# Linear attention and a two-layer MLP on one core: causal score blocks for seven pairs, one more pair in half-size products, and a new list of steps for the first stages

## The chip, the core and the metric

The kernel runs on one core of a Trainium2 chip. Its time is the device time of one execution in microseconds (us), the median of several runs; lower is better. The engines are named as in the profile: PE is TensorE's matrix unit and PEld its weight loads, DVE is VectorE, ACT is ScalarE, POOL is GpSimd, SP is SyncE, here a queue of transfers.

## The reference

Inputs `r`, `k`, `v` have shape (4, 8, 768, 48): batch, heads, time, head size. For every batch and head a 48 x 48 state is carried over time:

```
for t in range(S):
    kt, vt, rt = (k[:, :, t].copy(), v[:, :, t].copy(), r[:, :, t].copy())
    cur = np.einsum('bhd,bhe->bhde', u[None] * kt, vt)
    y[:, :, t] = np.einsum('bhd,bhde->bhe', rt, state + cur)
    state = w[None, :, :, None] * state + np.einsum('bhd,bhe->bhde', kt, vt)
```

The result, as 3072 tokens of 384 values, goes through `h = x @ w_in` (384 x 2048), `max(0.01 h, h)` and `@ w_out` (2048 x 384).

## The kernel before, in words

The 3072 tokens are 24 **stages** of 128, six to a batch (`NC`); two stages make a **pair** `m` (stages 2m and 2m+1). For each stage the recurrence is written as masked attention within the stage plus a product with the state that the stage before left.

- `prep` (letter P): r and k times powers of the decay (L318, or L325 and L327 for stages under 8). `turn` (T): PE transposes in eight matmuls (L388), ACT copies them out as `tp` (L395); from stage 8 on a DMA on SP's queue transposes (L320).
- `a_mm` (A): the scores, 128 x 128 for each of 8 heads, by `PE.matmul` (L408). Keys lie on PSUM's partitions, queries along the row; a head's 48 rows sit at partition 0 or 64, so two heads run on two halves of PE's rows. `a_mask` (M) masks them, with a product (L426) under stage 8, and from 8 on with a predicated copy (L418) into a tile that holds the diagonal already. That diagonal, the bonus `u`, comes from `bonuses` (B, L348 to L354) and `diag_tile`: on POOL (L370) for stages 8 to 11, on ACT (L376) from 12 (`LED`). Under stage 8 it comes through `diag` (X, L332) and `prep2` (Q, L340).
- `kv_mm` (K): k times v (L442); under stage 8 also the bonus columns (L438) and, as one matmul with the identity, the old state (L447). `state` (S): the new state, a product with the decay (L492), or from stage 8 on an addition and a product (L495, L497).
- `y_part` (Y): the stage's output, 16, 28 or 40 matmuls with 32 weight columns on four column groups (L527), copied to `xT` by ACT (L542).
- The first MLP product of a pair: eight groups J of six matmuls (`g1_pair`, L572), each with an ACT leaky ReLU (L578); stage by stage as G (L555).
- The second product: `g2` (H, L589) with 16 matmuls of 384 columns a stage; or `g2_seven`, which treats the pair's product as a 2 x 2 block product in seven half-size products of eight matmuls of 192 columns (L653) instead of eight, with sums of weights (`w_sum`, Z, L609) and of activations (`g_sum`, L627) on DVE, copies by ACT (L661, L677) and additions by DVE (L684). `SEVEN` holds the pairs treated so: 3 to 11.

The order of the work is written out. `ORDER` lists steps by letter and stage ("A4" is `a_mm(4)`), `LOADS` the loads that POOL's queue issues first (k, r, v of a stage, quarters of w_in and w_out). Then a loop over pairs m = 3 to 11 (`FIRST // 2` on) runs: J of pair m, scores and masks of stages 2m+4 and 2m+5, Y of 2m+2 and 2m+3, K, and the second product of pair m-1. `Sched.add` records each instruction with what it reads and writes; each engine plays its own in the order recorded and waits on semaphores for the others. Nothing is reordered at run time. PSUM's eight banks are handed out in turn by `next_bank`. F is a filler matmul, C, W, U and V prepare decay and bonus tables.

## Time and profile before

| what | value |
|---|---|
| time, median of 3 runs | 166.37 us (166.37 to 166.47) |
| span of the profiled execution, first to last instruction | 164.3 us |
| PE busy / PEld busy | 158.6 / 134.3 us |
| DVE busy / ACT busy / POOL busy | 124.1 / 120.5 / 77.0 us |
| share of the chain that ended last: PE / DVE / ACT | 93% / 4% / 1% |
| bytes moved by DMA | 19.68 MB |

The profile is one execution, and its own time is given as its span; the times are of executions without a profile. Busy time of PE counts a matmul from its start to its modelled end, and matmuls overlap, so 97% busy does not mean that no time is lost. The chain of waits follows the work back from the last instruction: each piece is what the next one had to wait for.

### The profile page before, as it was taken

The numbers are of one execution on the slowest core, as the hardware profiler recorded it, in microseconds if no ns is written. First come the engines' busy times: TensorE is split into PE (matmuls) and PEld (weight loads), VectorE is DVE, ScalarE is ACT, GpSimd is POOL, SyncE is SP. The second block draws the span as 40 slices with busy tenths as digits, with TensorE's granted clock in tenths as the row PEclk, the third lists the DMA queues.
The fourth block names the chain that finished last, engine by engine and source line by source line (L and its number), as shares of the span: only waits on it lengthen the run. The fifth ranks groups of instructions, "written<-read, shape, count | busy, mean of one in ns | idle before, by whom it ended". The sixth has DMA issues, their size and how long they took to land.

```text
span 164.3 us, 5453 instructions
## 1 busy us (share of the span) xinstructions
PE 158.6 (97%) x2315; PEld 134.3 (82%) x2315; DVE 124.1 (76%) x245; ACT 120.5 (73%) x285; POOL 77.0 (47%) x93
## 2 busy tenths in 40 slices
PE   5989899999999999999999999999999999999993
PEld 3858678788657875889889899899899899898993
DVE  7798938646999999986998997778989467045253
ACT  3767587789113869989989989989899836828530
POOL 7999999992099997750840921910000000000000
PEclk9999999999999999999999999999999999999999
DMA  4999999999999999999994995996208102002023
GB/s 96 127 152 166 172 150 171 179 196 145 148 124 246 114 126 102 214 169 84 178 128 80 195 103 110 157 110 133 90 4 193 34 4 96 4 7 89 4 96 96
DMA packets 99259, 19.68 MB, mean 120 GB/s; under 512 B 92322, under 2 KB 99236, under 8 KB 99236
## 3 DMA queue, kind: packets, MB, share of 16 engines
q0 software_dynamic: 76512, 10.03, 95.9%
q1 hardware_dynamic: 21682, 9.11, 27.5%
q8 instruction: 18, 0.29, 0.7%
q10 hardware_dynamic: 1042, 0.20, 0.6%
q14 instruction: 5, 0.04, 0.1%
HBM read 20.45 MB, written 4.72 MB: 153 GB/s over the span
## 4 chain that ended last, share of the span: by engine, by line
PE 93%; DVE 4%; ACT 1%; issue 0%
PE ps_all L572 37%; PE ps_all L653 26%; PE ps_all L589 10%; PE ps_all L527 7%; PE ps_all L408 4%; PE ps_all L388 2%; PE ps_all L442 2%; DVE at L426 2%; PE ps_all L254 1%; PE ps_all L294 1%; PE ps_all L466 1%; DVE vs L340 1%; ACT tp L395 1%; PE ps_all L555 1%; ACT gT L578 0%
## 5 line engine op out<-in xcount | busy, mean ns | idle before, releaser
L572 PE MATMUL ps_all<-xT,w_in_sb 128*128 128x256 bf16 x564 | 64.9, 273 | 0.0
L572 PEld LDWEIGHTS ps_all<-xT,w_in_sb 128*128 128x128 bf16 x564 | 54.3, 98 | 7.0 <-issue 0.2
L578 ACT ACTIVATE gT<-ps_all 128x512 bf16<-128x512 f32 x94 | 53.9, 596 | 5.8 <-PE ps_all L572 3.0
L217 POOL DMA_DIRECT2D rk_sb<-in_k_dram x23 | 21.3, 926 | 21.7 <-PE ps_all L572 21.7
L376 ACT ACTIVATE at<-ident,s_tok 128x128 bf16<-128x128 bf16 x96 | 30.4, 392 | 1.0 <-DVE s_tok L354 1.0
L418 DVE CAST_PREDICATED at<-mask,ps_all 128x1024 bf16<-128x1024 uint16 x16 | 18.8, 1220 | 5.3 <-PE ps_all L408 5.3
L217 POOL DMA_DIRECT2D v_sb<-in_v_dram x24 | 22.3, 934 | 0.8 <-POOLq L860 0.8
L684 DVE TENSOR_TENSOR out_sb<-ps_all,snap 128x192 f32<-128x192 f32 x28 | 9.9, 356 | 16.5 <-PE ps_all L653 15.8
L217 POOL DMA_DIRECT2D rk_sb<-in_r_dram x23 | 21.3, 926 | 0.0
L653 PE MATMUL ps_all<-tw,gs 128*128 128x192 bf16 x216 | 20.6, 246 | 0.0
L653 PEld LDWEIGHTS ps_all<-tw,gs 128*128 128x128 bf16 x216 | 18.1, 98 | 0.0
L589 PE MATMUL ps_all<-w_out_sb,gT 128*128 128x384 bf16 x96 | 16.4, 326 | 0.0
L653 PE MATMUL ps_all<-w_out_sb,gT 128*128 128x192 bf16 x144 | 14.9, 246 | 0.0
L627 DVE TENSOR_TENSOR gs<-gT 128x1024 bf16<-128x1024 bf16 x18 | 12.3, 684 | 2.9 <-ACT gT L578 2.9
L542 ACT ACTIVATE xT<-ps_all 128x384 bf16<-128x384 f32 x24 | 11.0, 492 | 4.2 <-PE ps_all L527 3.9
L589 PEld LDWEIGHTS ps_all<-w_out_sb,gT 128*128 128x128 bf16 x96 | 9.1, 98 | 5.8
L661 ACT ACTIVATE snap<-ps_all 128x192 f32<-128x192 f32 x27 | 9.0, 332 | 4.9 <-PE ps_all L653 4.3
L370 POOL TENSOR_TENSOR at<-ident,s_tok 128x512 bf16<-128x512 bf16 x8 | 8.7, 1131 | 7.5 <-DVE s_tok L354 7.5
L527 PE MATMUL ps_all<-at,v_sb 128*32 128x128 bf16 x384 | 11.9, 224 | 0.2 <-DVE vs L340 0.2
L653 PEld LDWEIGHTS ps_all<-w_out_sb,gT 128*128 128x128 bf16 x144 | 11.8, 98 | 0.3
L426 DVE TENSOR_TENSOR at<-ps_all,mask 128x512 bf16<-128x512 f32 x16 | 10.3, 685 | 2.1 <-PE ps_all L408 2.1
L527 PEld LDWEIGHTS ps_all<-at,v_sb 128*32 128x32 bf16 x384 | 9.1, 98 | 2.6 <-issue 0.9
(80 smaller groups left out, 220.0 us busy)
## 6 DMA issues: line engine op xcount, KB each, us to landing
out_dram<-out_sb SPq DMA_DIRECT2D x22, 192.0 KB, 2.3
v_sb<-in_v_dram POOLq DMA_DIRECT2D x24, 96.0 KB, 5.2
rk_sb<-in_r_dram POOLq DMA_DIRECT2D x23, 96.0 KB, 5.1
rk_sb<-in_k_dram POOLq DMA_DIRECT2D x23, 96.0 KB, 5.2
w_in_sb<-in_moe_w_in_dram POOLq DMA_DIRECT2D x4, 384.0 KB, 6.5
w_out_sb<-in_moe_w_out_dram POOLq DMA_DIRECT2D x4, 384.0 KB, 10.6
out_dram<-out_sb SPq DMA_DIRECT2D x4, 96.0 KB, 1.6
tp<-qk SPq DMA_TRANSPOSE x16, 3.7
```

Of the source, the lines that this page charges most:

```text
L217: add("pool", lambda: G.dma_start(dst, src), R=pace, W=[key], dma=f"{which}{n}")
L376: add("act", lambda h=h: A.activation(at[ia][:, h % 2, h // 2, :], ident[:, :], AF.Copy, scale=s_tok[n % 4][:, h:h + 1]), R=["ident", ("s" ...
L418: add("dve", lambda: V.copy_predicated(at[n % NAT][:, :, :, :].rearrange("p two m i -> p (two m) i"), mask[:, :].bitcast(mybir.dt.uint16). ...
L426: add("dve", lambda hh=hh, part=part: V.tensor_tensor(at[n % NAT][:, hh, :, :], part, mask[:, :].unsqueeze(1).to_broadcast([128, NP, 128]) ...
L527: last = PE.matmul(ps_y[32 * q:32 * q + 32, 128 * s:128 * s + 128], a, m, start=first_mm, stop=last_mm)
L542: add("act", lambda: A.activation(xT[m % NX][:, :, 128 * half:128 * half + 128], ps_y[:, 0:HD].rearrange("p (s t) -> p s t", t=128), AF.Copy),
L572: last = PE.matmul(ps_g[:, 256 * f:256 * f + 256], w_in_sb[:, s, 128 * fb:128 * fb + 128], xT[ix][:, s, :], start=s == 0, stop=s == NSL - 1)
L578: add("act", lambda: A.activation(gT[ig][:, 2 * j:2 * j + 2, :].rearrange("p f t -> p (f t)"), ps_g[:, :], AF.Prelu, alpha=0.01), R=[key], ...
L589: last = PE.matmul(ps_o[:, 0:HD], gT[ig][:, s, 128 * half:128 * half + 128], w_out_sb[:, s, :], start=s == 0, stop=s == NFB - 1)
L627: add("dve", lambda: V.tensor_tensor(x[i][:, :, :], a, b, op), R=keys, W=[("gs", m % 2, i)])
L653: done = PE.matmul(ps_o[:, 0:NH], lhs[:, s, :], rhs[:, s, :], start=first and s == 0, stop=s == HF - 1, skip_group_check=not (first and last))
L684: add("dve", lambda: V.tensor_tensor(out_sb[io][:, cols], ps_o[:, 0:NH], snap[i2][i][:, :], ALU.add), R=[key, ("snap", i2, i), *after], W= ...
```

## The change

Seven things change.

1. **Scores in causal blocks.** For the pairs (8, 9), (10, 11) to (20, 21) the odd stage is held with its two halves of 64 tokens exchanged (`SWAPPED`). Its loads and its stores become two half transfers each, and it gets its own decay table and mask. `a_blocks` makes the scores of both stages in one run of 32 matmuls on four 64 x 64 tiles of PE (row half by head, column half by keys), leaving out the blocks in which no key comes before a query. In the stage in natural order the first 64 keys meet all 128 queries and the last 64 keys only 64; in the exchanged stage it is the other way round. The order of the 32 is written by a small reckoning with 9 an issue, 56 for a 128-query product and 29 for a 64-query one.
2. **Pair 2 in seven half-size products**, its steps placed singly in the list (N2.0 to N2.6, its sums O2.0 to O2.3).
3. **States added by VectorE**: stages under 8 take the addition and product too, but for stage 7, which keeps the identity matmul as a step of its own (R7).
4. **A new list** of steps, which now reaches through J of pair 3 and the second product of pair 2; the loop runs from m = 4. Halves of P, T and M are placed singly, and J groups in any order.
5. **A new list of loads**: k3 before r2, later stage 4, weights of w_out in another order; r and k of a stage are loaded apart from v (l, v).
6. **Diagonal tiles** of stages 8 and 9 are made by ACT (E), of 10 and 11 by POOL (D).
7. Stores of whole stages (I), a skip of banks (b), and the tables for exchanged stages (t, m) become steps.

The core of the diff; left out are the table allocations, the keys by halves, and steps that are only handed on:

```diff
@@ -21,13 +21,17 @@
 NFB = DFF // 128
 NSL = HD // 128
 
-FIRST, EARLY = 6, 2
-LOADS = """r1 k1 wi0 id r2 k2 tri v1 r3 k3 v2 wi1 k4 r4 v3 wi2 k5 r5 r6 k6 v4 v5 k7 wi3 r7 v6 v7 wo3 wo2 wo1 wo0"""
+FIRST, EARLY = 8, 2
+SWAPPED = (9, 11, 13, 15, 17, 19, 21)
+LOADS = """r1 k1 wi0 id k3 tri r2 k2 v1 r3 v2 wi1 v3 wi2 k4 r4 k6 k5 r5 r6 k7 v4 v5 wi3 v7 r7 v6 wo0 wo2 wo1 wo3"""
 ORDER = """
-P0 C F1 T0 P1 F1 T1.0 A0 T1.1 X0 M0 K0 W F1 V A1 Q0 X1 S0 Y0 M1 G0.0 K1 P2 T2 Q1 P3 Y1 T3 S1 X2 A2 M2 K2 G1.0 X3 A3 U J0.2 S2 Q2 M3 Y2 K3 P4
-T4 Q3 J0.3 S3 Y3 J0.4 J0.5 J1.0 P5 A4 J1.1 P6 X4 M4 T5 X5 J1.2 K4 Q4 A5 S4 T6 J1.3 K5 J1.4 Y4 M5 L8 Q5 Y5 P7 J1.5 A6 J0.6 J2.0 J2.1 T7 M6 X6
-X7 K6 J2.2 J2.3 A7 S6 J2.4 J2.5 L9 Q6 J0.7 J1.6 J2.6 M7 Z0 Z1 Z2 L10 J2.7 L11 J1.7 K7 S7 P8 Q7 P9 B8.9 H0 K8 H1 P10 L12 K9 H2 S8 S9 Y6 Y7 A8
-A9 P11 M8 H3 M9 L13
+F1 P0.0 P0.1 C T0.0 T0.1 X0 A0 F1 K0 P1.0 F1 W M0.1 P1.1 T1.1 M0.0 Q0 T1.0 Y0 A1 P3.1 G0.0 S0 P2.0 X1 T2.0 P2.1 K1 M1.0 M1.1 T3.1 Q1 P3.0 T2.1 Y1 S1
+T3.0 X2 A2 M2.0 X3 G1.0 M2.1 A3 V K2 J0.3 Q2 M3.1 J0.2 S2 M3.0 K3 Y2 l8.3 J0.5 Q3 P4.1 P4.0 S3 P5.1 U Y3 P6.1 T4.1 T4.0 J0.4 J1.2 A4 P5.0 T5.1 J1.3
+M4.1 P6.0 X4 M4.0 T5.0 J1.4 T6.1 J1.1 X5 K4 J1.0 K5 v8.3 P7.1 Q4 T6.0 A5 S4 Y4 T7.1 J1.7 M5.1 M5.0 Q5 P7.0 X6 J0.6 Y5 v9.25 l9.33 A6 T7.0 v10.31 M6.1
+K6 J2.5 A7 M6.0 J0.7 Q6 S6 M7.1 J2.2 J2.0 J2.1 J2.6 X7 J2.4 M7.0 t l10.22 K7 Z0 Z2 Z1 P8 J1.5 J1.6 J2.3 J2.7 Q7 Z3 B8.9 E8.4.5 v11.33 E9.2.3 l11.20 H1
+m H0 R7 P9 E8.2.3 S7 I1 H2 O2.0 Y6 l12.2 E8.0.1 E9.0.1 E9.4.5 O2.2 Y7 K9 K8 O2.1 P10 S8 P11 E8.6.7 H3 l13.32 J3.4 S9 B10.11 E9.6.7 A8 M8 J3.3 D10 M9
+J3.7 O2.3 J3.0 I0 J3.1 B12.13 v13.22 v12.24 D11 I3 J3.6 J3.2 I2 l14.30 J3.5 E12.0.1 l15.40 A10 Y8 M10 P13 E13.6.7 Y9 P12 N2.0 N2.1 E13.4.5 K10 v14.24
+N2.2 S10 E13.0.1 b1 N2.3 E12.2.3 E12.4.5 N2.4 v15.24 E13.2.3 N2.5 M11 E12.6.7 N2.6
 """
 
 
...
@@ -138,8 +142,13 @@
     NQK, NTP, NVS, NAT, NT, NX, NG, NO, NRK = 6, 6, 6, 6, 6, 3, 3, 4, 14
     TURNED, DIAG = 8, 8
     LED = 12
-    SEVEN = (3, 4, 5, 6, 7, 8, 9, 10, 11)
+    SEVEN = (2, 3, 4, 5, 6, 7, 8, 9, 10, 11)
     HF, NH = NFB // 2, HD // 2
+    HL = L // 2
+    SWAP = SWAPPED
+
+    def swapped(n):
+        return n in SWAP
     w_in_sb = SB("w_in_sb", [128, NSL, DFF])
     w_out_sb = SB("w_out_sb", [128, NFB, HD])
     rk_sb = SB("rk_sb", [128, NRK, 2, HD])
...
@@ -213,8 +226,18 @@
...
-        key = (which, n if which == "v" else n % NRK)
-        add("pool", lambda: G.dma_start(dst, src), R=pace, W=[key], dma=f"{which}{n}")
+        slot = n if which == "v" else n % NRK
+        if swapped(n):
+            for half in range(2):
+                to, of = slice(HL * half, HL * half + HL), slice(HL - HL * half, L - HL * half)
+                add("pool", lambda to=to, of=of: G.dma_start(dst[to], src[of]), R=pace, W=[(which, slot, half)],
+                    dma=f"{which}{n}{half}")
+            return
+        add("pool", lambda: G.dma_start(dst, src), R=pace, W=[(which, slot, 0), (which, slot, 1)], dma=f"{which}{n}")
+
+    def got(which, n):
+        slot = n if which == "v" else n % NRK
+        return [(which, slot, 0), (which, slot, 1)]
 
     def load_stage(n, pace=()):
         for which in "krv":
...
@@ -358,13 +391,10 @@
         for step in range(3):
             for n in stages:
                 bonus(n, step)
-        for n in stages:
-            if n < LED:
-                diag_tile(n)
 
     def diag_tile(n, heads=range(H)):
         ia = n % NAT
-        if n < LED:
+        if heads is None:
             for hh in range(2):
                 s_of = s_tok[n % 4][:, :].rearrange("p (m two) -> p two m", two=2)[:, hh, :]
                 add("pool", lambda hh=hh, s_of=s_of: G.tensor_tensor(
...
@@ -399,6 +429,9 @@
         it = n % NTP
         if n >= DIAG and taken[0] % 8 == 7:
             taken[0] += 1
+        if swapped(n + 1):
+            a_blocks(n)
+            return
         at_bank[n] = (next_bank(), next_bank())
 
         def emit():
...
@@ -411,17 +444,48 @@
...
-    def a_mask(n):
+    def a_blocks(n):
+        stages = (n, n + 1)
+        for x in stages:
+            if taken[0] % 8 == 7:
+                taken[0] += 1
+            at_bank[x] = (next_bank(), next_bank())
+
+        def block(x, p, hh, half):
+            rows, keys = slice(64 * hh, 64 * hh + D), slice(HL * half, HL * half + HL)
+            whole = half == (1 if swapped(x) else 0)
+            queries = slice(0, L) if whole else keys
+            dst = at_bank[x][hh][0][keys, 128 * p + queries.start:128 * p + queries.stop]
+            return PE.matmul(dst, tp[x % NTP][rows, NP + p, keys], tp[x % NTP][rows, p, queries], start=True, stop=True)
+
+        def emit():
+            now, free = 0, {(hh, half): 0 for hh in range(2) for half in range(2)}
+            todo = {tile: [(x, p) for p in range(NP) for x in stages] for tile in free}
+            while any(todo.values()):
+                def turn_of(tile):
+                    return max(free[tile], now) + 2 * (tile[1] == swapped(todo[tile][0][0])), tile[0]
+
+                tile = min((t for t in todo if todo[t]), key=turn_of)
+                x, p = todo[tile].pop(0)
+                start = max(free[tile], now)
+                now, free[tile] = start + 9, start + (56 if tile[1] == swapped(x) else 29)
+                last = block(x, p, *tile)
+            return last
+
+        add("pe", emit, R=[("tp", x % NTP, half) for x in stages for half in range(2)],
+            W=[key for x in stages for _, key in at_bank[x]])
+
+    def a_mask(n, *parts):
...
-                mask[:, :].bitcast(mybir.dt.uint16).unsqueeze(1).to_broadcast([128, H, 128]),
+                (mask_s if swapped(n) else mask)[:, :].bitcast(mybir.dt.uint16).unsqueeze(1).to_broadcast([128, H, 128]),
...
-                R=[key for _, key in at_bank[n]] + ["mask"] + halves, W=halves)
+                R=[key for _, key in at_bank[n]] + (["mask_s"] if swapped(n) else ["mask"]) + halves, W=halves)
             return
-        for hh in range(2):
+        for hh in parts or range(2):
...
...
@@ -443,17 +507,18 @@
                                      qk[iq][:, H + 2 * p:H + 2 * p + 2, :].rearrange("p h e -> p (h e)"),
                                      v_sb[:, n, :].rearrange("p (h e) -> p h e", e=E)[:, 2 * p:2 * p + 2, 0:D],
                                      start=p == 0 or not carried, stop=not carried)
-            if live and carried:
-                last = PE.matmul(ps_kv[:, 0:HD], ident[:, :], st[n % NT][:, :, :].rearrange("p m e -> p (m e)"),
-                                 start=False, stop=True)
             return last
 
-        reads = [("kp", iq), ("v", n), ("qk0", iq)]
+        reads = [("kp", iq), ("qk0", iq)] + got("v", n)
         if n < DIAG:
             reads += [("prod", n % 4), "wu0", "wu1"]
-        if live and carried:
-            reads += [("st", n % NT), "ident"]
         add("pe", emit, R=reads, W=[key])
+
+    def carry(n):
+        ps_kv, key = kv_bank[n]
+        add("pe", lambda: PE.matmul(ps_kv[:, 0:HD], ident[:, :], st[n % NT][:, :, :].rearrange("p m e -> p (m e)"),
+                                    start=False, stop=True),
+            R=[("st", n % NT), "ident"], W=[key, ("carried", n)])
 
     def decay_columns():
         ps_c, key_c = next_bank()
...
@@ -590,10 +655,19 @@
...
+        add("pe", emit, R=[("gT", ig, half, j) for j in range(8)] + [("wout", i) for i in range(4)], W=[key, ("second", n)])
...
+
+    def g2_store(n):
+        io = n % NO
+        if swapped(n):
+            for half in range(2):
+                of, to = HL * half, 128 * n + HL - HL * half
+                add("sp", lambda of=of, to=to: SP.dma_start(out[to:to + HL, :], out_sb[io][of:of + HL, :]),
+                    R=[("o", io, 0), ("o", io, 1)], W=[("out", n, half)], dma=f"o{io}")
+            return
         add("sp", lambda: SP.dma_start(out[128 * n:128 * n + 128, :], out_sb[io][:, :]),
             R=[("o", io, 0), ("o", io, 1)], W=[("out", n, 0)], dma=f"o{io}")
 
...
@@ -695,6 +771,15 @@
             for n, h in tiles[lo:hi]:
                 diag_tile(n, [h])
 
+        if step is not None:
+            [lambda: (product(0, (0, 0), (top, one), True, False), keep(0, 0)),
+             lambda: (product(1, 0, 0, True, False), keep(1, 1)),
+             lambda: (product(0, 1, 1, False, False), keep(0, 2)),
+             lambda: (product(2, (0, 1), (low, one), True, True), plus(2, 0, 0, 0)),
+             lambda: (product(0, 2, 2, False, False), plus(0, 1, 1, 1)),
+             lambda: (product(1, 3, (low, two), False, True), plus(1, 2, 0, 1)),
+             lambda: (product(0, (1, 1), 3, False, True), plain(0, 1, 0))][step]()
+            return
         if not final:
             product(0, (0, 0), (top, one), True, False)
             some(0, 2)
...
@@ -739,6 +824,22 @@
...
 
+    def swapped_tables():
+        for name, own, col, turned in (("q", "qexp", qexp, qexp_s), ("k", "kexp", kexp, kexp_s)):
+            for half in range(2):
+                rows = slice(HL * half, HL * half + HL)
+                by = float((HL if half == 0 else -HL) * (1 if name == "q" else -1))
+                add("dve", lambda rows=rows, by=by, col=col, turned=turned: V.tensor_scalar(
+                    turned[rows, :], col[rows, :], 1.0, by, ALU.mult, ALU.add), R=[own], W=[(own, "s", half)])
+        for i, (own, turned) in enumerate((("qexp", qexp_s), ("kexp", kexp_s))):
+            add("act", lambda i=i, turned=turned: A.activation(tab_s[:, i, :], lnw[:, :], AF.Exp, scale=turned[:, 0:1]),
+                R=[("lnw", 0), ("lnw", 1), (own, "s", 0), (own, "s", 1)], W=[f"tab_s{i}"])
+
+    def swapped_mask():
+        add("dve", lambda: V.tensor_copy(mask_s[:, :], mask[:, :]), R=["mask"], W=["mask_s"])
+        add("dve", lambda: V.memset(mask_s[0:HL, HL:L], 0.0), R=["mask_s"], W=["mask_s"])
+        add("dve", lambda: V.memset(mask_s[HL:L, 0:HL], 1.0), R=["mask_s"], W=["mask_s"])
+
...
...
@@ -748,8 +849,16 @@
...
-    steps = {"U": u_table, "V": u_cast, "P": prep, "Q": prep2, "B": bonuses, "T": turn, "A": a_mm, "M": a_mask, "K": kv_mm, "S": state, "Y": y_part, "X": diag, "C": decay_columns, "W": decay_table, "F": fill, "Z": w_sum,
-             "G": g1, "J": g1_pair, "H": g2, "L": lambda n: load_stage(n, pace=[("pace", (n - 4) // 2, (n - 4) % 2)])}
+    def load_paced(n, after, which="krv"):
+        for one in which:
+            load_one(n, one, pace=[("second", after) if after < 10 else ("pace", after // 10 - 1, after % 10)])
+
+    def skip_banks(n):
+        taken[0] += n
+
...
+             "G": g1, "J": g1_pair, "H": g2, "L": load_paced,
+             "l": lambda n, after: load_paced(n, after, "kr"), "v": lambda n, after: load_paced(n, after, "v")}
...
...
@@ -760,34 +869,29 @@
...
-
+                g2_store(2 * m + half)
+
+    while taken[0] % 8 != 6:
+        taken[0] += 1
...
-        first = [n for n in ahead if n < LED]
-        if first:
-            bonuses(*first)
-        if first and further:
-            w_sum(3)
-            bonuses(*further)
...
-        if further and not first:
+        if further:
             bonuses(*further)
-        for n in (2 * m + 8, 2 * m + 9):
-            if n < NST:
-                load_stage(n, pace=[("pace", 2 * m, 0)])
+        for which in ("kr", "v"):
+            for n in (2 * m + 8, 2 * m + 9):
+                for one in which * (n < NST):
+                    load_one(n, one, pace=[("pace", 2 * m, 0)])
         for n in ahead:
-            if n < DIAG:
-                diag(n)
+            if not swapped(n):
+                a_mm(n)
         for n in ahead:
-            a_mm(n)
-        if not first:
-            for n in ahead:
-                a_mask(n)
+            a_mask(n)
...
```

61 lines of the change are left out of this document (36 added, 25 removed).

## The prediction

> **What bounds the kernel now.** I read the page first, then the chain of waits in order of time, then groups by line and the timeline where a term needed them.
>
> ```profile
> span 164.3 us, 5453 instructions
> PE 158.6 (97%) x2315; PEld 134.3 (82%) x2315; DVE 124.1 (76%) x245; ACT 120.5 (73%) x285; POOL 77.0 (47%) x93
> PE 93%; DVE 4%; ACT 1%; issue 0%
> ```
>
> TensorE (PE) carries 93% of the chain. The chain itself shows where it does not (start, length, what):
>
> ```profile
> 13.13 0.18 PE ps_all L447
> ...
> 15.60 1.29 DVE at L426 x2
> ...
> 18.15 1.20 DVE at L426 x2
> ...
> 21.22 0.67 PE ps_all L527 x40
> ...
> 25.09 0.60 ACT gT L578
> 25.69 0.99 ACT tp L395 x2
> ...
> 40.72 0.08 PE ps_all L438 x4
> ...
> 40.99 0.16 PE ps_all L447
> 41.15 2.60 PE ps_all L589 x16
> ...
> 58.86 0.55 PE ps_all L408 x16
> ...
> 65.89 5.24 PE ps_all L572 x48
> ...
> 73.02 4.68 PE ps_all L653 x56
> ...
> 152.50 9.32 PE ps_all L653 x112
> ```
>
> The reader is to see two regions. From 27 us to 161.8 us the chain holds nothing but matmuls, so there a microsecond of matmul time taken out is a microsecond of the end, as long as no other engine takes over. Before 27 us it leaves PE several times, longest from 15.60 to the end of Q3's and P4's steps near 19.9, where VectorE (DVE) masks, scales and adds for stages 2 and 3 while PE has too little to do. The steady loop starts pair 4 at 65.89 in this kernel; the changed list of steps ends at the same point of the work (pairs 0 to 3 through the first product, pairs 0 to 2 through the second, scores to stage 11), so I compare the two up to that point and then per loop.
>
> The span is 164.3 us; the median time is 166.37 us, so 2.07 us lie outside the span, which I leave as they are.
>
> **The change part by part.**
>
> *Pair 2 in seven half-size products.* Two products of 16 matmuls each, 2 x 2.60 = 5.20 us, become seven of 8: the row at 73.02 gives 4.68 us. Term: **-0.52 us**. On the path. It brings four sums on DVE and three additions from PSUM:
>
> ```profile
> L627 DVE TENSOR_TENSOR gs<-gT 128x1024 bf16<-128x1024 bf16 x18 | 12.3, 684 | 2.9 <-ACT gT L578 2.9
> L684 DVE TENSOR_TENSOR out_sb<-ps_all,snap 128x192 f32<-128x192 f32 x28 | 9.9, 356 | 16.5 <-PE ps_all L653 15.8 <-ACT snap L661 0.7
> ```
>
> That is 4 x 0.68 + 3 x 0.36 = 3.8 us of DVE, to be hidden; see DVE below.
>
> *States added by VectorE.* The identity matmul that carried the state into PSUM (0.16 to 0.18 us in the chain) ran five times and stays once, for stage 7: 4 x 0.165 = **-0.66 us** of PE. Four times DVE does an addition and a product instead of one product:
>
> ```profile
> L447 PE MATMUL ps_all<-st,ident 128*128 128x384 bf16 x5 | 1.6, 326 | 0.0
> ...
> L495 DVE TENSOR_TENSOR sum_t<-ps_all,st 128x384 bf16<-128x384 f32 x11 | 6.1, 551 | 0.0
> ...
> L497 DVE TENSOR_TENSOR st<-sum_t,wl 128x384 bf16<-128x384 bf16 x11 | 4.3, 394 | 0.4
> ```
>
> The product alone is the 0.39 us that each costs DVE beyond the addition, which takes the place of the old product; three of them fall in the stretch before 22 us in which DVE is on the chain.
>
> *Causal blocks.* A pair's scores are 16 products of 128 queries (first row below), and become 32 products on four tiles: per tile four of 128 queries and four of 64. No row has a 64-wide tile; the nearest is L527, four 32-column tiles side by side:
>
> ```profile
> 58.79 0.62 PE L408 MATMUL ps_all<-tp 48*128 48x128 bf16 x16
> ...
> 59.63 0.23 PE L527 MATMUL ps_all<-at,v_sb 128*32 128x128 bf16 x4
> 59.69 0.23 PE L527 MATMUL ps_all<-tp,st 128*32 128x128 bf16 x4
> 59.74 0.23 PE L527 MATMUL ps_all<-at,v_sb 128*32 128x128 bf16 x4
> ```
>
> In the first row the last product alone lasts 0.22 us, so the starts of eight twos span 0.40: one two every 56 ns, 448 ns a pair. On L527 four products start every 55 ns, so four tiles work at once, their weight loads are hidden, and an issue costs no more than 14 ns. A 64-query product should take half, some 29 ns. A tile then needs 4 x 56 + 4 x 29 = 340 ns; products issue in order, and stepping through the written order with the 9 ns an issue that the new code itself reckons with ends it at 388 ns. Gain 448 - 388 = 60 ns, or 108 at best; I take 80 ns a pair: 7 x 0.08 = **-0.56 us**. Bounds: -0.76 us (nothing lost to issue) and +3.1 us (second rival). Masks, their number and their size stay; the products still sit between two other shapes, so the gaps around them stay too.
>
> [...]
>
> *Swapped loads.* In seven stages each load becomes two half loads, 21 more issues on POOL's queue, and each store of theirs two on SP's.
>
> ```profile
> L217 POOL DMA_DIRECT2D v_sb<-in_v_dram x24 | 22.3, 934 | 0.8 <-POOLq L860 0.8
> L231 POOL DMA_DIRECT2D w_out_sb<-in_moe_w_out_dram x4 | 3.0, 824 | 0.0
> ```
>
> A w_out issue has half the rows of a v issue (512 against 1024) and still takes 0.82 us, so a half load costs nearly a whole one: 21 x 0.7 = 15 us more on POOL, which is busy 77 of 164. All come after the weights. Cost nil; the cover is POOL's idle half. Without it a load lands late for a stage two pairs on.
>
> *DVE and the diagonal tiles.* Stages 8 and 9 get their diagonal tiles from ScalarE (ACT) and no longer from POOL.
>
> ```profile
> 40.25 0.96 DVE L609 TENSOR_TENSOR tw<-w_out_sb,tw 128x1536 bf16<-128x1536 bf16 x1
> ...
> 55.06 5.25 DVE L609 TENSOR_TENSOR tw<-w_out_sb,tw 128x1536 bf16<-128x1536 bf16 x1
> 55.41 4.08 POOL L370 TENSOR_TENSOR at<-ident,s_tok 128x512 bf16<-128x512 bf16 x4
> 40.00:45.00 5.00, 5.00 (x44) 3.38 (x43) 4.97 (x12) 1.74 (x4) 0.00 (x0) 1.00 2.64 146
> 45.00:50.00 5.00, 5.00 (x86) 3.20 (x87) 4.90 (x9) 1.14 (x3) 4.43 (x4) 1.00 1.42 164
> ```
>
> DVE's difference of weights stood 5.25 us while POOL made four tiles; the same form at 40.25 took 0.96 (first row). In the new list it comes before any POOL tile, so DVE gets back about 4.3 us, which pays for the 3.8 us of sums. The 16 ACT tiles fall where ACT is busy 1 to 2 of 5 us (after the window's length stand PE, PEld, DVE, ACT and POOL, each with its count). Still, counting DVE's steps from the weight differences to the end of the list gives some 24 us of work in 24.6 us: hidden, with little to spare. What PE waits for there (masks of stages 8 and 9, transposes of 8 to 11) is due 2 to 3 us before its turn.
>
> *The early list.* DVE decides up to step Q3, which lets Y3 go:
>
> ```profile
> 8.63 1.29 DVE L426 TENSOR_TENSOR at<-ps_all,mask 128x512 bf16<-128x512 f32 x2 [0.35 <-PE ps_all L408]
> ...
> 17.61 0.55 DVE L340 TENSOR_TENSOR vs<-v_sb,ps_all 128x384 bf16<-128x384 bf16 x1
> 18.07 1.28 DVE L426 TENSOR_TENSOR at<-ps_all,mask 128x512 bf16<-128x512 f32 x2
> 19.27 0.35 DVE L325 TENSOR_TENSOR qk<-rk_sb,tab 128x384 bf16<-128x384 bf16 x1
> ...
> 19.81 0.56 DVE L340 TENSOR_TENSOR vs<-v_sb,ps_all 128x384 bf16<-128x384 bf16 x1
> 20.28 0.55 DVE L492 TENSOR_TENSOR st<-ps_all,wl 128x384 bf16<-128x384 f32 x1
> ```
>
> From the first mask at 8.63 to the end of Q3, where the next row starts at 20.28, DVE hardly rests; the starts give what a step takes of the queue (a mask pair 1.20, a scaling 0.47, a pair of decay products 0.54, a state 0.47). In the new list the steps from the first mask to Q3 are 4 x 1.20, 4 x 0.47, 3 products of L332 x 0.33, 3 x 0.54, and states 0.47 + 2 x 0.86: 11.5 us, so 20.1, and an estimated 0.4 us more because k3 and k2 land just when their steps are due. That is 20.5, about as late as before. But three J groups stand ahead of Y3 and not two (0.66 us of PE under the wait), the scores of stage 1 fill the wait for xT, and at 26 us, where ACT held the chain for 1.59 us, more J is at hand. Against this stage 4's r is loaded a place later behind k4:
>
> ```profile
> 23.34 0.36 DVE L325 TENSOR_TENSOR qk<-rk_sb,tab 128x384 bf16<-128x384 bf16 x1 [2.51 <-DMA rk_sb<-in_r_dram]
> 39.26 0.96 DVE L609 TENSOR_TENSOR tw<-w_out_sb 128x1536 bf16<-128x1536 bf16 x1 [1.38 <-DMA w_out_sb<-in_moe_w_out_dram]
> ```
>
> The loads land in a row without a break (stage 5 waited until 23.34), so in the new list stage 4 is complete near 21.8 and PE idles about 0.45 us for its transposes. Following PE's steps from Y3 (end near 21.3 instead of 21.89) to the first second product I get 39.7 instead of 41.15; 0.66 of that are the state products counted above and 0.16 the one that now comes later, so 0.6 is left: **-0.5 us** for the list. Bounds: -2.0 (nearly half of the stretch of 4.3 us at 15.60) and +1.2 us (three times 0.39 us with no J under it). It cannot gain much more: the w_out weights land near 39.2 (second row), and no second product can start before.
>
> **Sum:** -0.52 - 0.66 - 0.56 - 0.5 = -2.24 us; span 162.1, time 166.37 - 2.24 = **164.1 us**.
>
> **The rivals.**
>
> 1. *The blocks gain nothing.* A 64-query product takes as long as a 128-query one (its load shows): 8 x 56 ns a tile, as now. For it: no row has a 64-wide load. Time 166.37 - 0.52 - 0.66 - 0.5 = 164.7. [...]
>
> 2. *The loads of the tiles share one path* (the other side). Four 32-column loads fit in 55 ns, at most 13.9 ns each; if that is because they queue, a 64-column load takes 27.7 ns and 32 of them 0.89 us, +0.44 us a pair, +3.1 us in all: 166.37 - 1.68 + 3.1 = 167.8. Slower from +0.24 us a pair on, 21.5 ns a product. Against it: rows 0 to 63 and 64 to 127 of the scores already load side by side, and a two-column product with a full load takes 20 ns (40.72, four in 0.08).
>
> 3. *The early list loses.* The extra additions and a late load put Y1 to Y3 behind without J to fill: +1.2 instead of -0.5: 165.8. For it: DVE has no slack from 8.6 to 20.3 us.
>
> 4. *The list gains more*, nearly half of the stretch at 15.60: -2.0 instead of -0.5: 162.6. Against it: the weights' landing.
>
> 5. *DVE takes over between 40 and 65 us.* 24 us in 24.6 us; 2 us of stalls (POOL's four tiles stand in its way again) reach the path after the slack: +1 us, 165.1.
>
> **How the numbers follow.** Forecast 0.44, rival 1 0.14, rival 2 0.11, rival 3 0.12, rival 4 0.11, rival 5 0.08. A measurement of this kernel tells about 0.2% (0.33 us) from no change. Faster: the forecast, 1, 4, 5 and most of 3, less a share for two of them together: 0.80; same 0.05; slower 0.15. The range leaves out rival 2 and half of rival 4: 162.8 to 166.3.
>
> **What would show it.** Chain: one L447-like step; second products 5.20 us gone before the loop. Scores of stages 12 and on: about 0.47 us a pair where 0.55 stood; 0.55 means rival 1, 0.9 or more rival 2. Loop start of pair 4 near 64.1 instead of 65.89; later than 65.9 means rival 3 or 5, and the chain says where: DVE pieces before 27 us (3) or after 40 us (5). The forecast is wrong if the chain after 27 us holds more than 1 us that is not PE.

## The result, and the profile after

The changed kernel takes **168.66 us** (median of 6 executions, 168.04 to 169.66), the kernel before 166.42 beside it: 1.0141 times as long, 95% interval 1.0106 to 1.0177. A second measurement, on another chip, gave 1.0144 (1.0090 to 1.0198). Ratios, here and below, are of the means of fast executions, so they are not quite the quotients of the medians. The forecast was 164.1 with a range up to 166.3: wrong by 4.6 us, and on the wrong side.

The profiled execution took 168.14 us, of which the span is 166.4. Three lines of its page, the span, the engines, and the shares of the chain of waits:

```profile
span 166.4 us, 5784 instructions
...
PE 157.3 (95%) x2447; PEld 135.0 (81%) x2447; DVE 127.1 (76%) x263; ACT 125.4 (75%) x305; POOL 83.0 (50%) x110
...
PE 83%; DVE 5%; POOL 4%; DMA 3%; issue 2%; ACT 2%; POOLq 0%; DVEq 0%
```

PE's busy time fell by 1.3 us, from 158.6, but PE now carries 83% of the chain and not 93%. The chain in order of time (start, length, what) says where it left PE:

```profile
18.09 0.67 issue
...
24.25 0.32 issue
...
40.94 5.20 PE ps_all L654 x32
...
54.64 2.35 DVE at L482 x2
...
58.11 2.62 DVE ku L381 x2
...
61.00 0.62 DVE ku L384 x2
61.62 0.47 DVE s_tok L387
...
64.41 3.54 PE ps_all L731 x40
67.95 5.24 PE ps_all L637 x48
73.19 0.47 PE ps_all L459 x31
```

Three points of the work, the same in every kernel, cut the span into stretches: the first second product (40.94), the start of pair 4 in the loop (67.95), and the end of the last addition. The last two columns are kernels of the experiments below. All rows but the last are of one profiled execution each: 166.3 us in the column of the mended orders, 165.3 in the last.

| us | before | forecast | changed | all orders mended | the same, 38 instructions more |
|---|---|---|---|---|---|
| first second product | 41.15 | 39.7 | 40.94 | 41.92 | 41.02 |
| from there to pair 4 | 24.74 | 24.4 | 27.01 | 24.21 | 24.22 |
| pair 4 to the last addition's end | 96.31 | 95.9 | 95.96 | 95.96 | 95.95 |
| from there to the span's end | 2.1 | 2.1 | 2.5 | 2.4 | 2.4 |
| time, median | 166.4 | 164.1 | 168.7 | 165.8 | 164.8 |

So the loop gave what was forecast; 1.2 us are missing ahead of the first second product and 2.6 between there and the loop. (0.4 us more lie behind the last addition, in the stores' landing; no run was made for them.) Why the second stretch grew stands in three views. PE's waits (total, times, longest; the two rows with issue belong to the first stretch and come further below):

```profile
PE ps_all L506 <- DVE at L482: 2.1, 1, 2.1
...
PE ps_all L637 <- issue: 0.7, 1, 0.7
PE ps_all L441 <- issue: 0.3, 1, 0.3
```

L506 is K10, the state product of stage 10. It waits for a mask although it reads none: its PSUM bank is the one in which the scores of stage 10 stood (bank 7, by the order in which banks are handed out), and the mask M10 reads them. DVE's instructions in order of time show why that mask is late:

```profile
58.11 2.96 DVE L381 TENSOR_TENSOR ku<-rk_sb,u_tab 128x384 bf16<-128x384 bf16 x2
61.00 0.62 DVE L384 TENSOR_TENSOR ku<-rk_sb,ku 128x384 bf16<-128x384 bf16 x2
61.54 1.00 DVE L387 TENSOR_REDUCE s_tok<-ku 128x8 f32<-128x384 bf16 x2
62.46 1.21 DVE L482 CAST_PREDICATED at<-mask,ps_all 128x1024 bf16<-128x1024 uint16 x1
```

Step B12.13, six instructions for stages that are due a pair later, stands ahead of M10 in DVE's queue, and its first two products together take 2.96 us where the next two of the same size take 0.62. POOL in the same stretch (idle time before an instruction and what ended it, in brackets):

```profile
49.31 0.89 POOL L236 DMA_DIRECT2D rk_sb<-in_k_dram  x1 [8.39 <-PE ps_all L654]
...
58.65 2.21 POOL L400 TENSOR_TENSOR at<-ident,s_tok 128x512 bf16<-128x512 bf16 x2
60.81 0.95 POOL L236 DMA_DIRECT2D rk_sb<-in_k_dram  x1
```

While POOL makes the diagonal tiles of stage 11 (58.65 to 60.86), DVE's two products take nearly five times as long. The loads that B12.13 needs are issued from 49.31 on, held back 8.39 us by their gate (step H2, the second product of stage 2, the first of pair 1), and the last half of r of stage 13 lands at 60.70. So two causes end together at 60.7 to 60.9. Which of them counts was the first question.

### The profile page after: what moved, and what is told of

The parts are those of the page before. It is cut to its first block, busy times and chain, and to the rows that moved or that the text cites. A ratio compares the mean times of both kernels' runs of the same rounds, so it can differ in the third digit from the quotient of the medians.

```text
span 166.4 us, 5784 instructions
## 1 busy us (share of the span) xinstructions
PE 157.3 (95%) x2447; PEld 135.0 (81%) x2447; DVE 127.1 (76%) x263; ACT 125.4 (75%) x305; POOL 83.0 (50%) x110
## 4 chain that ended last, share of the span: by engine, by line
PE 83%; DVE 5%; POOL 4%; DMA 3%; issue 2%; ACT 2%; POOLq 0%; DVEq 0%
PE ps_all L637 34%; PE ps_all L731 28%; PE ps_all L592 6%; PE ps_all L654 6%; DMA rk_sb<-in_k_dram 3%; PE ps_all L506 2%; POOL rk_sb L236 2%; PE ps_all L441 2%; DVE ku L381 2%; PE ps_all L418 2%; PE ps_all L459 1%; DVE at L482 1%; ACT at L406 1%; DVE at L490 1%; POOL v_sb L236 1%
## 5 line engine op out<-in xcount | busy, mean ns | idle before, releaser
L637 PE MATMUL ps_all<-xT,w_in_sb 128*128 128x256 bf16 x564 | 65.2, 273 | 0.7 <-issue 0.7
L406 ACT ACTIVATE at<-ident,s_tok 128x128 bf16<-128x128 bf16 x112 | 35.6, 390 | 4.9 <-DVE s_tok L387 4.9
L236 POOL DMA_DIRECT2D rk_sb<-in_k_dram x16 | 14.8, 926 | 24.6 <-PE ps_all L637 16.2
L731 PE MATMUL ps_all<-tw,gs 128*128 128x192 bf16 x240 | 23.1, 246 | 0.3 <-ACT snap L739 0.3
L731 PEld LDWEIGHTS ps_all<-tw,gs 128*128 128x128 bf16 x240 | 20.0, 98 | 0.5 <-ACT snap L739 0.5
L236 POOL DMA_DIRECT2D v_sb<-in_v_dram x17 | 16.2, 960 | 0.8 <-POOLq L961 0.8
L731 PE MATMUL ps_all<-w_out_sb,gT 128*128 128x192 bf16 x160 | 16.5, 247 | 0.0
L482 DVE CAST_PREDICATED at<-mask,ps_all 128x1024 bf16<-128x1024 uint16 x9 | 10.9, 1220 | 5.5 <-PE ps_all L459 3.2
L236 POOL DMA_DIRECT2D rk_sb<-in_r_dram x16 | 14.8, 929 | 0.0
L731 PEld LDWEIGHTS ps_all<-w_out_sb,gT 128*128 128x128 bf16 x160 | 13.0, 98 | 0.5
L425 ACT ACTIVATE tp<-ps_all 128x512 bf16<-128x512 f32 x16 | 9.1, 601 | 2.8 <-PE ps_all L418 2.8
L654 PE MATMUL ps_all<-w_out_sb,gT 128*128 128x384 bf16 x64 | 10.9, 326 | 0.0
L233 POOL DMA_DIRECT2D v_sb<-in_v_dram x14 | 10.3, 791 | 0.0
```

The source lines that it names most:

```text
L236: add("pool", lambda: G.dma_start(dst, src), R=pace, W=[(which, slot, 0), (which, slot, 1)], dma=f"{which}{n}")
L406: add("act", lambda h=h: A.activation(at[ia][:, h % 2, h // 2, :], ident[:, :], AF.Copy, scale=s_tok[n % 4][:, h:h + 1]), R=["ident", ("s" ...
L482: add("dve", lambda: V.copy_predicated(at[n % NAT][:, :, :, :].rearrange("p two m i -> p (two m) i"), (mask_s if swapped(n) else mask)[:, ...
L637: last = PE.matmul(ps_g[:, 256 * f:256 * f + 256], w_in_sb[:, s, 128 * fb:128 * fb + 128], xT[ix][:, s, :], start=s == 0, stop=s == NSL - 1)
L654: last = PE.matmul(ps_o[:, 0:HD], gT[ig][:, s, 128 * half:128 * half + 128], w_out_sb[:, s, :], start=s == 0, stop=s == NFB - 1)
L731: done = PE.matmul(ps_o[:, 0:NH], lhs[:, s, :], rhs[:, s, :], start=first and s == 0, stop=s == HF - 1, skip_group_check=not (first and last))
```

## Experiments between the first second product and the loop

The theory: place in a queue is the whole of it, B12.13 ahead of M10. The rival: DVE, POOL and the DMA engines have too much to do there, and another wait takes the place of each that goes. Edits are to the list of steps unless said otherwise; ratios are to the kernel before on the same chip.

**Loads earlier, tiles earlier, both.** Gate of the loads of 12 and 13 moved from H2 to H1, which runs first of all second products (a); POOL's tiles D11 ahead of two loads of v (b); both (c).

```diff
-O2.0 Y6 l12.2 E8.0.1                     (a, c)
+O2.0 Y6 l12.1 E8.0.1
-B12.13 v13.22 v12.24 D11 I3              (b, c)
+B12.13 D11 v13.22 v12.24 I3
```

> The changed kernel with k and r of stage 12 (and so of 13 behind them on POOL's queue) released by the second-product step H1 instead of H2. My theory: in the changed kernel step B12.13 stands on VectorE until 61 us for two reasons that end together, the last half load of r13 (lands 60.7) and POOL's two diagonal tiles of stage 11 (58.65 to 60.86); mask M10 stands behind it, K10 on PE behind M10 by its bank (2.1 us) and the third of pair 2's seven products behind ACT (0.3 us). Taking away the load alone leaves POOL's tiles: I expect the loop of pair 4 to start where it did (67.95, within 0.5 us) and 168.1 to 168.7 us. If the load alone held B12.13: start near 65.7, time near 166.3. If VectorE is simply full: unchanged, 168.1 to 168.7.

> The changed kernel with POOL's diagonal tiles of stage 11 ahead of the v loads of stages 13 and 12 on POOL's queue. My theory: the tiles then run from about 56.4 to 58.5 us, under the masks of stages 8 and 9, and hold B12.13's first product no longer, but r13 still lands near 60.7: loop start unchanged within 0.5 us, 168.0 to 168.7 us. If POOL's tiles alone held VectorE: start near 65.8, time near 166.4. If VectorE is simply full: unchanged.

> Both edits: loads of stages 12 and 13 released by H1, and POOL's tiles of stage 11 ahead of the v loads. My theory (two causes that end together): only now does B12.13 run at 57 to 59.5 us; M10 follows A10 at once, K10 waits no more than 0.7 us, the loop of pair 4 starts at 65.5 to 66.2 instead of 67.95, time 166.0 to 166.8 us. If one of the two alone was the cause, the time here equals that of the run that removed it. If VectorE is simply full, start at 67 or later and 167.5 or more.

a: 170.37 us, ratio 1.0207 (1.0123 to 1.0291), above the 168.1 to 168.7 expected, because PE's clock was halved for a while in three of its four executions (mean granted clock 0.99; see under hardware); loads issued from 44.57 instead of 49.31, yet the two products of L381 take 2.96 us again, under POOL's tiles, and K10 waits 2.1 us. b: 168.17, 1.0136 (1.0066 to 1.0206); the two take 1.46, but the last L384 starts only at 61.38, behind the load of r13, whose last half lands at 61.30, and K10 waits 1.7. c: 168.40, 1.0116 (1.0058 to 1.0174); K10's wait is 0.4 and pair 4 starts near 66.7 (65.5 to 66.2 was expected, and 166.0 to 166.8 us). Either cause alone holds the mask; both must go. But c's next pair starts at 80.25, where the changed kernel had 79.69. DVE's queue in c:

```profile
73.30 0.36 DVE L384 TENSOR_TENSOR ku<-rk_sb,ku 128x384 bf16<-128x384 bf16 x1 [2.28 <-DMA rk_sb<-in_r_dram]
```

r15 came late. POOL issued the loads of 14 and 15 from 61.64, behind its tiles, and not from 60.81; the last half of r15 was issued 0.75 us later than in the changed kernel, and it landed 4.1 us later (73.22 for 69.14). Why it took so much longer is not shown. The gain was given back one pair on, as the rival has it.

**The mask first** (d): B12.13 behind M10 and the decay products, the ACT tiles that need it further back.

```diff
-J3.1 B12.13 v13.22 ... A10 Y8 M10 P13 E13.6.7 Y9 P12 N2.0 N2.1 E13.4.5 K10
+J3.1 v13.22 ... A10 Y8 M10 P13 Y9 P12 B12.13 N2.0 N2.1 K10
```

> The changed kernel with step B12.13 and the diagonal tiles of stages 12 and 13 put behind mask M10, P13 and P12 in the list (tiles on ACT behind the copy of the third of pair 2's products). Loads and POOL's order as in the changed kernel. My theory (M10 and the copies are held by what stands ahead of them in their queues): K10 waits under 0.5 us, the loop of pair 4 starts at 65.2 to 65.8 instead of 67.95; of these 2.3 us up to 1 us may be given back in the next loop, where ACT then makes 16 tiles before the first group's copies. Time 165.9 to 167.0 us. If VectorE is simply full: M10 still ends after 62 us and the time stays at 167.8 or more.

167.16 us, ratio 1.0042 (1.0018 to 1.0066): 1.0% below the changed kernel by a few steps moved, with no load, no POOL tile and no operation changed. M10 starts at 59.99, as soon as its scores are there, and K10's wait is gone; pair 4 starts at 66.77, later than the 65.2 to 65.8 asked. The next two rows are DVE's, the last is of PE's waits:

```profile
59.99 1.22 DVE L482 CAST_PREDICATED at<-mask,ps_all 128x1024 bf16<-128x1024 uint16 x1 [1.37 <-PE ps_all L459]
61.46 0.56 DVE L348 TENSOR_TENSOR qk<-rk_sb,tab_s 128x768 bf16<-128x768 bf16 x1 [0.24 <-DMA rk_sb<-in_r_dram]
```

```profile
PE ps_all L731 <- DVE out_sb L761: 0.9, 1, 0.9
```

The theory holds for the largest part. What stays is 0.9 us: DVE idles 1.37 us ahead of the mask, then takes the decay products that waited for r13, then B12.13, and the additions that free a PSUM bank come behind them.

**Loads of 14 and 15 earlier too** (e: c and this; f: d, a and this, with P13 P12 ahead of the mask and D11 ahead of the loads of v). The expectation of f calls the gates of a the first and the second half of pair 1's product; they are H1, of pair 0, and H2.

```diff
-H3 l13.32 J3.4 ... I2 l14.30 J3.5 E12.0.1 l15.40 A10
+H3 l13.32 l14.30 l15.40 J3.4 ... I2 J3.5 E12.0.1 A10
```

> The kernel with both edits (earlier loads of stages 12 and 13, POOL's tiles ahead of two loads of v) and a third: the loads of r and k of stages 14 and 15 come directly behind those of 12 and 13. If what took back the 1.3 us was only the late loads of 14 and 15 (r15 landed at 73.2 us), DVE's wait of 2.28 us for r15 goes, the next pair's first products start near 79.0 instead of 80.08, and the time is about 166.9 instead of 168.4. If it was the transposes of stages 12 and 13, started at 62.97 behind the bonus step, the wait of 1 us of the scores of stage 12 stays and the time stays within 0.4 us of 168.4.

> The order with the mask of stage 10 ahead of the bonus step (167.16 before), and beside it: loads of 12 and 13 gated by the first instead of the second half of the product of pair 1, loads of 14 and 15 behind them, POOL's tiles ahead of the loads of v, and the decay products of 13 and 12 ahead of the mask. By the theory that queue positions alone made the loss after 41 us, the remaining gap of 1.17 us on PE at 64.8 goes (the products of 13 no longer wait for r13 until 61.27), pair 4 starts near 65.6 and the time is near 165.9, below the kernel before by about 0.5 us. By the rival that DVE has too much to do between 41 and 65 us, another wait of about 1 us takes its place and the time stays near 167.

e: 167.55, ratio 1.0060 (1.0022 to 1.0098); f: 167.55, 1.0065 (1.0017 to 1.0113). In e the late r15 and K10's wait are gone and the next pair starts at 78.70, close to the 79.0 expected, though the time missed its 166.9; f missed its 165.9 by 1.6 us. Both have a new wait of PE, here in e, ahead of the scores of stages 10 and 11:

```profile
60.51 0.59 PE L459 MATMUL ps_all<-tp 48*64 48x64 bf16 x32 [1.68 <-issue]
```

The view names no releaser. By the landing times in the trace it is the DMA transposes of stage 11, on which these scores wait too: issued at 51.90 they landed at 60.42, 8.5 us later, and in f they took 8.6 (52.38 to 61.00). In the changed kernel it was 6.8 (51.90 to 58.71), and in the loop, where POOL issues no load from 75.8 to 80.8, 3.0 (77.10 to 80.15). The profile counts the packets of transposes and loads alike as shares of the same 16 DMA engines. Over all 16 transposes of e:

```profile
DMA to landing us min/median/max: 3.0/3.7/8.9
```

**Transposes earlier** (h: e, and P11 ahead of S8 on DVE), **all orders mended** (i).

```diff
-O2.1 P10 S8 P11 E8.6.7                   (h, i)
+O2.1 P10 P11 S8 E8.6.7
-J3.1 B12.13 v13.22 v12.24 D11 I3 J3.6 J3.2 I2 l14.30 J3.5 E12.0.1 l15.40 A10 Y8 M10 P13 ...   (i: also l12.1)
+J3.1 D11 l14.30 l15.40 v13.22 v12.24 I3 J3.6 J3.2 I2 J3.5 P13 P12 A10 Y8 M10 Y9 B12.13 ...
```

> The kernel with earlier loads of 12 to 15 and POOL's tiles ahead of two loads of v, and one edit more: the decay products of stage 11, behind which their transposes are issued, stand ahead of the state addition of stage 8 on DVE. In the kernel without it PE had a gap of 1.95 us before the scores of stages 10 and 11 that the trace gives no cause for; the transposes of stage 11 were issued at 51.90 and landed at 60.42, 8.5 us later, where transposes without loads beside them land after 3.0 us. By the theory that transposes share the DMA engines with the loads, issuing them about 1.7 us earlier takes most of that gap away (below 0.6 us) and the start of pair 4 moves from 66.96 to about 65.4: time about 166.0. If the gap is another thing (instructions arriving late, the banks), it stays at 1.9 us and the time is unchanged, 167.5.

> Everything together: mask of stage 10 ahead of the bonus step, loads of 12 and 13 earlier, decay products of stage 11 earlier, POOL's tiles and then the loads of 14 and 15 ahead of the loads of v. By the theory that the loss after 41 us is the place of a few steps on DVE, POOL and the DMA queues, no wait above 0.5 us is left on PE between 41 us and the loop, pair 4 starts 2.3 us earlier than in the changed kernel (about 65.6), and the time is 166.0, 0.4 below the kernel before. By the rival that DVE or the DMA engines are simply full in this stretch, a wait of about 1 us remains somewhere and the time stays at 167.

h: 166.98, ratio 1.0024 (0.9990 to 1.0058). The gap is 1.36 us from product to product (1.95 in e) where below 0.6 was expected, and the time 166.0: the transposes of stage 11 were issued 0.8 us earlier and landed at 60.43, as in e. Issued sooner, with four stages' loads ahead of them, they landed no sooner. In i those of 14 and 15 come behind POOL's tiles; the transposes issued at 51.47 land at 57.22, and no wait is left. i: **165.80, ratio 0.9945 (0.9917 to 0.9974)**, and on a second chip 165.84, 0.9947 (0.9919 to 0.9976). Its shares of the chain, and its chain:

```profile
PE 95%; issue 1%; ACT 1%; DVE 1%
```

```profile
41.92 5.20 PE ps_all L654 x32
...
59.81 0.47 PE ps_all L459 x32
...
62.77 3.37 PE ps_all L731 x40
66.13 5.24 PE ps_all L637 x48
```

From 41.92 to the last addition everything on the chain is PE, and the stretch to pair 4 takes 24.21 us. The rival is refuted: all operations of the changed kernel fit, none taken out, in another order. Beside it the changed kernel ran on that second chip (control o, 168.91), and the 1.4 to 2.0% asked of it were 1.9 by the medians, two of its six executions with the halved clock.

> The kernel with all orders mended, unchanged, as the control on the chip of the two kernels above: 165.8, ratio to the kernel before 0.9945, if what was measured holds on another chip.

> The changed kernel unchanged, as the control on the same chip: ratio to the kernel before 1.014 as measured; by the theory that its loss after 41 us is three waits that the mended orders take away, 1.4 to 2.0% above the kernel with all orders mended.

## Experiments ahead of the first second product

**A load** (g): k of stage 2 loaded ahead of k of stage 3, and stage 3's decay products behind the masks of stage 1.

```diff
-... id k3 tri r2 k2 v1 r3 ...            (loads)
+... id k2 tri r2 k3 v1 r3 ...
-A1 P3.1 G0.0 S0 P2.0 X1 T2.0 P2.1 K1 M1.0 M1.1 T3.1 Q1 P3.0 T2.1 Y1 S1 T3.0
+A1 P2.1 G0.0 S0 P2.0 X1 T2.0 K1 M1.0 M1.1 T2.1 Q1 P3.1 P3.0 Y1 T3.1 S1 T3.0
```

> The changed kernel with k of stage 2 loaded ahead of k of stage 3, and the decay products of stage 3 behind the masks and the scaling of stage 1 on DVE. By the theory that the early chain hangs on the load of k2 (landing at 12.28 us, masks right behind it), the second output product Y1 starts near 13.9 instead of 14.38; if the early stretch passes that on, the first second product starts at 40.5 instead of 40.94 and the time is 168.2 instead of 168.66. By the rival that DVE's queue and not a load sets Y3, Y1 is earlier but Y3 is not, and the time stays within 0.2 us.

170.07, ratio 1.0186 (1.0118 to 1.0255): a miss, three of its four executions with the halved clock. Y1 starts at 14.86 and not at 13.9, and PE's nameless gap grew from 0.95 to 1.22 us. No gain is seen, but the changed kernel itself has Y1 at 14.38 in one profile and at 15.03 in another (control o), as its loads land sooner or later; so one profile doesn't settle what the exchange is worth.

**The nameless gaps.** In every kernel with the new list but one (m, below) PE stops once or twice with nothing that releases it, inside a group of like products. The rows of the changed kernel, of i, of s and of l (the next experiments), in that order, each from its own view of PE:

```profile
18.76 0.71 PE L637 MATMUL ps_all<-xT,w_in_sb 128*128 128x256 bf16 x5 [0.67 <-issue]
...
24.56 0.23 PE L441 MATMUL ps_all<-tp 48*128 48x128 bf16 x2 [0.32 <-issue]
```

```profile
19.74 0.70 PE L637 MATMUL ps_all<-xT,w_in_sb 128*128 128x256 bf16 x5 [1.35 <-issue]
```

```profile
23.57 0.27 PE L418 MATMUL ps_all<-ident,qk 128*128 128x128 bf16 x2 [0.96 <-issue]
```

```profile
23.02 0.22 PE L418 MATMUL ps_all<-ident,qk 128*128 128x128 bf16 x1 [0.39 <-issue]
```

Counted in the trace's instructions of PE (weight loads, products, and the waits of its sequencer), they stand at 448 to 450 and 704 to 707 in every kernel that has them, 256 apart. The trace also holds instruction loads, 16,384 bytes each, in the page of the changed kernel this row (count, MB, share of 16 engines):

```profile
q8 instruction: 19, 0.31, 0.7%
```

256 instructions to a load make 64 bytes an instruction. If PE's instructions come in blocks, adding some early moves each gap to other work. s adds 20 two-column products (40 instructions) to the changed kernel after step C; l puts the same 20 in i in place of a filling product of the same length (0.69 us at 4.19 for 0.61 at 4.18; the expectation has 1.65 us, a misreading of the row), 38 more; m 34 of them, 66 more.

```diff
-F1 P0.0 P0.1 C T0.0 T0.1                 (l; m: f34)
+f20 P0.0 P0.1 C T0.0 T0.1
+    def small(n):   # "f": n products of 128x128 ones by two columns
```

> The changed kernel with 20 two-column products of ones put in on PE near 4.5 us, where it waits; 40 instructions of PE more ahead of everything that follows, no other change. The two gaps of PE at 17.82 us (945 ns) and 24.03 us (532 ns) end with nothing the trace names. If they are PE's instructions arriving late, they stay at the same count of instructions and so come 40 instructions earlier in the work: before the scores and state products near 16.6 to 17 us, and near 22.9 us, and none inside the groups where they stood; the time may change by up to 1.3 us either way. If they belong to the work there (operands, banks), they stay at the same products.

> The kernel with all orders mended, and in place of the first filling product (2 instructions) 20 two-column products of ones (40 instructions), at 1.65 us where PE waits for w: 38 instructions of PE more ahead of all that follows, no time of their own on the way. In all kernels so far the work passed PE's instruction 704 between 5.79 and 6.15 us after 448, whatever stood there, and the first second product came 16.38 us after 704 in the eight kernels with the new list and no instruction put in; the start of the first 16 KB instruction load varied from 13.76 us (with 40 instructions put in) to 17.43. By the theory that PE's instructions arrive in blocks of 256 and that this sets the stretch from 18 to 25 us, the first gap (1.62 us in the kernel it is made from) moves off J's products and may vanish, a gap before instruction 704 stays, 704 comes 5.8 to 6.1 us after 448, and the time moves by up to 0.7 us, most likely down to 165.2. By the rival that the gaps belong to the work, both stay at the same products and the time stays at 165.8.

> The same with 34 small products, 66 instructions more. They take some 0.9 us from 1.65 us on, as the two products they stand for did with their gaps, or 0.3 us more. By the theory of blocks of instructions: gaps, if any, at instruction 448 and 704 again, which is 66 instructions earlier in the work (near 16.1 and 22 us in the changed kernel); 448 to 704 again 5.8 to 6.1 us; time 165.0 to 166.3. By the rival: gaps at the old products, time 165.8 to 166.1.

| us | goes on at 448 (after a stop of) | at 704 (after) | those two loads start | time, ratio |
|---|---|---|---|---|
| before | 17.74 (none) | 24.02 (none) | 15.48, 21.23 | 166.42 |
| changed | 18.76 (0.95) | 24.56 (0.53) | 16.43, 21.98 | 168.66, 1.0141 |
| i | 19.74 (1.62) | 25.54 (0.53) | 17.34, 23.06 | 165.80, 0.9945 |
| i, second chip | 18.32 (0.31) | 24.40 (0.81) | 15.91, 21.66 | 165.84, 0.9947 |
| s | 17.51 (none) | 23.57 (1.18) | 13.76, 20.69 | 169.88, 1.0145 (1.0049 to 1.0240) |
| l | 17.52 (none) | 23.02 (0.60) | 12.70, 20.12 | **164.77, 0.9883 (0.9848 to 0.9919)** |
| m | 17.83 (none) | 22.88 (none) | 12.13, 19.63 | 165.40, 0.9913 (0.9878 to 0.9949) |

(Stops are from one product's start to the next.) The gaps went with the count: in s, l and m none stands inside J's products any more, and where one is left it stands at 704, now in the transposes. That they belong to the count and not to the work is shown. Every stop of the table ended 2.3 to 2.9 us after its load started, so late instructions are the likely cause; that a load's late start is due to the full DMA queues of that phase is only argued. The fixed 5.8 to 6.1 us from 448 to 704 that l and m were expected to keep fell (5.5 and 5.05): blocks have no fixed pace. What the stops cost: l takes 1.07 us less than i on the same chip (164.62 to 165.34 against 165.09 to 166.18), more than the 0.6 expected of it. (The profiles are not the medians: l's took 165.34, its longest time, that of i on this chip 165.09, its shortest.) m has no stop at all and is no faster than l: its second output product Y1 came at 16.31, after l's 15.29, behind a load of k that landed at 14.21 (12.29 in the changed kernel). Counted from Y1, the stops account for the rest: to the first second product it takes 25.2 us in m, 25.7 in l, 26.6 in the changed kernel and 27.2 in i, and with their stops taken off (0, 0.60, 1.48 and 2.15) 25.1 to 25.2 in all four.

The same 20 products in the kernel before, which has no such stop:

```diff
-P0 C F1 T0 P1
+P0 C f20 T0 P1
```

> The kernel before with the filling product at 5.66 us (2 instructions) replaced by 20 two-column products (40 instructions, some 0.15 us more). In its profile no gap stood at PE's instructions 448 and 704, so by the theory that late instructions cost time only where PE comes to the end of a block early, nothing is gained: ratio to the kernel before 0.998 to 1.002. If the small products help by something else (a warmer clock, say), it gains about 0.6% as the other kernel did: 0.994.

166.86, ratio 0.9979 (0.9938 to 1.0020): most likely nothing, though the interval doesn't exclude a gain as in l.

## Experiments on single terms

**Whole scores** (j) in place of the blocks, in all seven pairs; swapped loads stay. **Carried states back on PE** (k) for stages 1 to 4.

```diff
-        if swapped(n + 1):
-            a_blocks(n)
-            return
-Y1 S1 ... S2 M3.0 ... S3 P5.1 ... S4 Y4
+Y1 R1 S1 ... R2 S2 M3.0 ... R3 S3 P5.1 ... R4 S4 Y4
```

> The changed kernel with whole score products (16 of 128 queries a pair) in place of the blocks; swapped loads, masks and tables stay. By the forecast's term (0.08 us a pair, seven pairs, five of them behind the start of the loop) scores take 0.55 us a pair again and the time is 0.4 to 0.56 us longer, about 169.1. By the rival that blocks gain nothing the time stays at 168.66 (with whole products ending no later).

> The changed kernel with the state carried into PSUM by an identity product on PE again for stages 1 to 4: four PE products of 0.165 us back, four scalings of 0.39 us off DVE. By the forecast's term the time is 0.66 us longer, 169.3. By the rival that DVE and not PE sets the stretch before 22 us, DVE's three products there (1.2 us) come off the way to the third output product, Y3 starts up to 1 us earlier and the time is 0.3 to 0.8 us shorter, 168.1.

j: 171.01, ratio 1.0230 (1.0165 to 1.0295), worse than the changed kernel, as the term says. (The list and the loop of j have A9, A11 and the other odd stages again.) Its time is more than 0.5 us above for the reason told under hardware; the clean figure is its chain, where a pair's scores are back at 0.55 us and pair 4 to pair 11 takes 81.53 us against 81.02:

```profile
75.73 0.55 PE ps_all L438 x16
```

k: 170.06, ratio 1.0184 (1.0128 to 1.0240). The first second product comes at 42.28, against 41.55, 41.92 and 41.89 in h, i and j, which share the early list, on the same chip: 0.36 to 0.73 us later. The stops differ, 1.34 us in k and 1.50 to 2.15 in the others; counted from Y1 and with the stops taken off, k takes 1.0 us more than each of the three. So the sign is clear, the size is not. DVE's three scalings less gained nothing: Q3 ends at 22.28, against 21.02 to 21.31 in the three, so the rival (fewer scalings let Y3 start earlier) falls.

## Why the prediction was wrong, step by step

- *Pair 2 in seven, -0.52*: right. With the waits gone (i) the stretch takes 24.21 instead of 24.74; the two pairs of blocks in it (-0.16) and the state product that moved into it (+0.16) cancel.
- *States added by VectorE, -0.66*: right in sign; k shows 0.36 to 0.73 as it stands and 1.0 with the stops taken off.
- *Causal blocks, -0.08 a pair*: right. 0.47 for 0.55; the loop became 0.35 us shorter for five pairs. 32 products in 0.47 us start every 14.7 ns, each with a load of 64 columns; of these loads, 108 ns each by their mean, 32 stand within 0.41 us from 73.12 in the changed kernel, so they overlap. Rivals 1 (0.55 us a pair) and 2 (0.89) both fell.
- *The early list, -0.5*: wrong. DVE kept the time that was worked out (Q3 ends at 20.44, forecast 20.5; 20.4 to 21.3 in other profiles of this list, as the loads land, so the hit is partly luck). The step that failed is "following PE's steps from Y3 ... I get 39.7": it took PE to run whenever operands were there. Y3 ended at 22.11 and not near 21.3, behind the first of two stops of 0.95 and 0.53 us; the second came after it. Together they are 1.3 us beyond what the products there take, and 1.24 lie between 39.7 and 40.94. The count from Y1 above shows that the stretch lengthens by just its stops. Rival 3 had the place (later by a late start), not the cause.
- *Swapped loads, "cost nil"*: not tested alone. The half loads do come after the weights, but on POOL's queue they stand between its tiles from 49 to 66 us, and the last half of r13, landed at 60.70, is one of the two things that hold B12.13. In i, with all half loads in place, no wait is left, so any cost depends on the order. Transposes are slow beside loads in the kernel before too (7.4 us from 50.61), so that is not the halves' doing.
- *DVE, "hidden, with little to spare ... due 2 to 3 us before its turn"*: wrong, and the largest part (2.6 us). DVE's steps were added up as if only their durations counted, and the list of what PE waits for names the masks of stages 8 and 9, not that of 10, for which PE waited 2.06 us. Left out were the order in which M10 stands behind B12.13, what POOL's tiles do to a DVE product beside them (a row of 5.25 us for 0.96 was quoted, for the place it had before), when r13 lands, and that a PSUM bank makes a product wait for a mask it doesn't read. Rival 5 named the mechanism, DVE between 40 and 65 us with POOL's tiles in its way again, but at 1 us and with a chance of 0.08.

The last sentence of the forecast's tests did its work: more than 1 us that is not PE after 27 us on the chain.

## What to carry to other kernels

In a list written by hand, ask of every wait what stands ahead of the releasing instruction on its own queue, and give work that is due later its place behind; busy time in a window says nothing of that. A wait can come through a PSUM bank, so know which product gets whose bank. Two causes that end within 0.2 us of each other must be taken away together before either shows, and a fix is judged one pair further on, where moved loads meet transposes. The best version (l) is the changed kernel with its steps reordered and its PE instructions shifted against the blocks: 1.2% below the kernel before.
